# Linear attention on one core: half of relu(k) moved to GpSimd, its v copy in 32-bit elements, and new queue orders

## The chip, the cores and the metric

One core of one Trainium2 chip. The time is the device time of one execution in microseconds, the median of several runs. "Span" is the time from the first to the last instruction in the profile; in every run here whose time and span are both listed the span is 1.8 us shorter than the time. Engines: PE (TensorE), DVE (VectorE), ACT (ScalarE), POOL (GpSimd), SP (which issues the DMAs). The program gives each engine a queue of its own, and semaphores order the engines among themselves. A run is called slow when it is over 1.5% above the fastest of the same kernel, and fast otherwise.

## The reference

```python
# q, k, v: (1, 32, 2048, 128) bf16, so 32 heads of 2048 x 128
phi_q = where(q > 0, q + 1, exp(q)) + 1e-6
phi_k = where(k > 0, k + 1, exp(k)) + 1e-6
kv  = einsum("bhsd,bhse->bhde", phi_k, v)
z   = einsum("bhsd->bhd", phi_k)
num = einsum("bhqd,bhde->bhqe", phi_q, kv)
den = einsum("bhqd,bhd->bhq", phi_q, z)[..., None] + 1e-6
return num / den
```

Both kernels write phi(x) as relu(x) + (min(exp(x), 1) + 1e-6) and never add the two parts: each part has its own matmul, and both accumulate in PSUM. A column of ones beside v makes z come out of the same matmuls as kv.

## The kernel before

Per head h (16 tiles of 128 rows): exp of k on ACT (`ek`), min/add on DVE (`em`), relu of k on DVE (`rk`), a copy of v beside the ones on GpSimd (`v1`), 32 k-v matmuls (`kv`), a copy of kv out of PSUM on ACT (`kvs`). q is transposed on PE into PSUM (`T`), ACT takes exp (`eq`) and half of relu (`rqa`), DVE the other half (`rqb`) and min/add (`emq`). The numerator matmuls (`nA`, `nC`) use kvs; DVE takes the reciprocal of the denominator (`r`) and the product (`f`). DVE reads PSUM in `rqb`, `r` and `f`; `em`, `rk` and `emq` go from SBUF to SBUF.

```python
def emrk(h):
    s = h % 2
    add("DVE", f"em{h}", lambda e: e.tensor_scalar(
        em_sb[:, s], em_sb[:, s], 1.0, EPS, op0=ALU.min, op1=ALU.add), [f"ek{h}"])
    add("DVE", f"rk{h}", lambda e: e.tensor_scalar(
        rk_sb[:, s], k_sb[:, h % NI], 0.0, None, op0=ALU.max), [f"ldk{h}"] + ([f"kv{h - 2}"] if h >= 2 else []))

def v1(h):            # waits: ldv{h}, kv{h - 2}, nA{h - 3}
    ...
    add("POOL", f"v1{h}", lambda e: e.tensor_scalar(
        v1_sb[:, h % 2, :, 0:D], v_sb[:, h % NI].rearrange("p (j d) -> p j d", d=D), 1.0, 0.0,
        op0=ALU.mult, op1=ALU.add), dep)
# ... (rqa takes half of relu(q) in three heads of four, all of it in the fourth)
for i in range(NH):                   # the order of every queue
    eq(i)
    ...                               # the first head has its own order
        rqa(i)
    if i + 1 < NH:
        kvs(i + 1)
    if i + 2 < NH:
        ek(i + 2)
    if i >= 1:
        f(i - 1, "A")                 # reciprocal and product of tiles 0 to 11
    rqb(i)
    emq(i)
    if i >= 1:
        f(i - 1, "C")                 # of tiles 12 to 15
    if i + 2 < NH:
        emrk(i + 2)
    if i + 1 < NH:
        T(i + 1)
    nA(i)
    nC(i)
    if i + 2 < NH:
        kv(i + 2)
```

Of the kernel before, what the change touches and what calls it, by code (L numbers as in the profile page):

```python
# [8 lines left out]
ENGINES = ("PE", "DVE", "ACT", "POOL", "SP")  # L9

# [5 lines left out]
class Program:  # L16



    def __init__(self, sem):  # L20
        self.sem = sem
        self.ops = {e: [] for e in ENGINES}
        self.where = {}
        self.count = {}
        self.sems = {}

    def add(self, eng, key, fn, deps=(), dma=None, inc=True):

        name = dma if dma is not None else eng
        if dma is not None or inc:  # L30
            self.count[name] = self.count.get(name, 0) + (16 if dma is not None else 1)
        if key is not None:
            assert key not in self.where, key
            assert dma is not None or inc
            self.where[key] = (name, self.count[name], eng, len(self.ops[eng]))
        self.ops[eng].append((fn, tuple(deps), name, (16 if dma is not None else 1) if (dma is not None or inc) else 0))
# [47 lines left out]
def _eps_pieces():  # L84

    import struct

    def bf(x):
        u = struct.unpack("<I", struct.pack("<f", x))[0]
        u = (u + 0x7FFF + ((u >> 16) & 1)) & 0xFFFF0000  # L90
        return struct.unpack("<f", struct.pack("<I", u))[0]

    a = bf(EPS / 128)
    b = bf(EPS - 126 * a)
    return a, b, bf(EPS - 126 * a - b)


def bass_standalone__linear_attn_elu__prompt_kernel(nc: bass.Bass, q: bass.AP, k: bass.AP, v: bass.AP, out: bass.AP):
    B, H, S, D = q.shape
    assert D == P and S == 16 * P  # L100
    NT = S // P
    NH = B * H
    bf16, fp32 = mybir.dt.bfloat16, mybir.dt.float32
    N = NT * D
    NC = D + 1
    NI = 8
    NO = 6
    LAG = 2
# [4 lines left out]
    with ExitStack() as es:  # L113
# [11 lines left out]
        k_sb, q_sb, v_sb = sb([P, NI, N]), sb([P, NI, N]), sb([P, NI, N])  # L125
        em_sb, rk_sb = sb([P, 2, N]), sb([P, 2, N])
        v1_sb = sb([P, 2, NT, NC])
        emq_sb, rq_sb = sb([P, 2, N]), sb([P, 2, N])
        kvs_sb = sb([P, 2, NC])
        rden_sb = sb([P, 2, NT], fp32)  # L130
        o_sb = sb([P, NO, NT, D])
        ident, ones, epsr, one1 = sb([P, P]), sb([P, P]), sb([P, 3]), sb([P, 1])
        xT = alloc(nc.psum_tensor, [P, N], bf16)
# [3 lines left out]
        CO = 4 * 512  # L137

        def slot(t):
            if t < 12:  # L140
                return 512 * (t // 3) + NC * (t % 3)
            return CO + 512 * ((t - 12) // 2) + NC * ((t - 12) % 2)

        pr = Program(sem)
        add = pr.add


# [9 lines left out]
        for s in range(2):  # L157
            add("DVE", f"v1ones{s}", lambda g, s=s: g.memset(v1_sb[:, s, :, D:NC], 1.0))


        def load(name, dst, src, h, freed):
            dep = [f"{f}{h - NI}" for f in freed] if h >= NI else []
            add("SP", f"ld{name}{h}", lambda e: e.dma_start(
                dst[:, h % NI].rearrange("p (j d) -> p j d", d=D), rows(src, h)), dep, dma=f"{name}{h % NI}")

        def loads(h):
            load("k", k_sb, kf, h, ["ek", "rk"])
            load("q", q_sb, qf, h, ["T"])
            load("v", v_sb, vf, h, ["v1"])

        def store(h):
            s = h % NO
            if h < NH - 1:
                add("SP", f"st{h}", lambda e: e.dma_start(rows(of, h), o_sb[:, s]), [f"fA{h}", f"fC{h}"], dma=f"o{s}")
            else:
                add("SP", None, lambda e: e.dma_start(rows(of, h)[:, 0:12, :], o_sb[:, s, 0:12]), [f"fA{h}"], dma=f"o{s}")
                add("SP", f"st{h}", lambda e: e.dma_start(rows(of, h)[:, 12:NT, :], o_sb[:, s, 12:NT]), [f"fC{h}"],
                    dma=f"o{s}")

        for h in range(min(NI, NH)):  # L180
            loads(h)
        for h in range(NH + LAG):
            if h + NI < NH:
                loads(h + NI)
            if h >= LAG:
                store(h - LAG)


        def ek(h):
            add("ACT", f"ek{h}", lambda e: e.activation(em_sb[:, h % 2], k_sb[:, h % NI], ACT.Exp),  # L190
                [f"ldk{h}"] + ([f"kv{h - 2}"] if h >= 2 else []))

        def eq(h):
            add("ACT", f"eq{h}", lambda e: e.activation(emq_sb[:, h % 2], xT[:, :], ACT.Exp),  # L194
                [f"T{h}"] + ([f"nC{h - 2}"] if h >= 2 else []))

        def split(h):
            return h % 4 != 3

        def rqa(h):  # L200
            n = N // 2 if split(h) else N
            add("ACT", f"rqa{h}", lambda e: e.activation(rq_sb[:, h % 2, 0:n], xT[:, 0:n], ACT.Relu),  # L202
                [f"T{h}"] + ([f"nC{h - 2}"] if h >= 2 else []))

        def rqb(h):
            if split(h):
                add("DVE", f"rqb{h}", lambda e: e.tensor_scalar(  # L207
                    rq_sb[:, h % 2, N // 2:], xT[:, N // 2:], 0.0, None, op0=ALU.max),
                    [f"eq{h}"] + ([f"nC{h - 2}"] if h >= 2 else []))

        def rqs(h):
            return [f"rqa{h}"] + ([f"rqb{h}"] if split(h) else [])

        def kvs(h):
            add("ACT", f"kvs{h}", lambda e: e.activation(kvs_sb[:, h % 2], kv_ps, ACT.Copy),  # L215
                [f"kv{h}"] + ([f"nC{h - 2}"] if h >= 2 else []))

        def emrk(h):
            s = h % 2
            add("DVE", f"em{h}", lambda e: e.tensor_scalar(  # L220
                em_sb[:, s], em_sb[:, s], 1.0, EPS, op0=ALU.min, op1=ALU.add), [f"ek{h}"])
            add("DVE", f"rk{h}", lambda e: e.tensor_scalar(  # L222
                rk_sb[:, s], k_sb[:, h % NI], 0.0, None, op0=ALU.max), [f"ldk{h}"] + ([f"kv{h - 2}"] if h >= 2 else []))

        def emq(h):
            s = h % 2
            add("DVE", f"emq{h}", lambda e: e.tensor_scalar(  # L227
                emq_sb[:, s], emq_sb[:, s], 1.0, EPS, op0=ALU.min, op1=ALU.add), [f"eq{h}"])

        def v1(h):  # L230
            dep = [f"ldv{h}"]
            if h >= 2:
                dep += [f"kv{h - 2}"]
            if h >= 3:
                dep += [f"nA{h - 3}"]
            add("POOL", f"v1{h}", lambda e: e.tensor_scalar(  # L236
                v1_sb[:, h % 2, :, 0:D], v_sb[:, h % NI].rearrange("p (j d) -> p j d", d=D), 1.0, 0.0,
                op0=ALU.mult, op1=ALU.add), dep)

        def T(h):  # L240
            def f(e):
                for j in range(NT):
                    ins = e.transpose(xT[:, j * P:(j + 1) * P], q_sb[:, h % NI, j * D:(j + 1) * D], ident[:])  # L243
                return ins
            add("PE", f"T{h}", f, [f"ldq{h}", "ident"] + (([f"eq{h - 1}"] + rqs(h - 1)) if h else []))

        def kv(h):
            def f(e):
                for j in range(NT):
                    for part, src in ((0, em_sb), (1, rk_sb)):  # L250
                        ins = e.matmul(kv_ps, lhsT=src[:, h % 2, j * D:(j + 1) * D], rhs=v1_sb[:, h % 2, j, :],  # L251
                                       start=(j + part == 0), stop=(j == NT - 1 and part == 1))
                return ins
            add("PE", f"kv{h}", f, [f"em{h}", f"rk{h}", f"v1{h}", "v1ones0", "v1ones1"] + ([f"kvs{h - 1}"] if h else [])
                + ([f"fC{h - 3}"] if h >= 3 else []))

        def num(h, tiles, bank, n, e):
            s = h % 2
            e.matmul(_ap(o_ps[:, :], slot(tiles[0]) + D, [[NC, n]]), lhsT=ones[:], rhs=epsr[:, 0:n], start=True, stop=False,  # L259
                     skip_group_check=True)  # L260
            for t in tiles:
                o = o_ps[:, slot(t):slot(t) + NC]
                e.matmul(o, lhsT=emq_sb[:, s, t * P:(t + 1) * P], rhs=kvs_sb[:, s, :], start=False, stop=False,  # L263
                         skip_group_check=True)
                ins = e.matmul(o, lhsT=rq_sb[:, s, t * P:(t + 1) * P], rhs=kvs_sb[:, s, :], start=False, stop=True,  # L265
                               skip_group_check=True)
            return ins

        def nA(h):
            def f(e):  # L270
                for b in range(4):
                    ins = num(h, range(3 * b, 3 * b + 3), b, 3, e)
                return ins
# [3 lines left out]
        def nC(h):  # L277
            def f(e):
                num(h, (12, 13), 4, 2, e)
                return num(h, (14, 15), 5, 2, e)  # L280
# [126 lines left out]
```

## Time and profile before

| | before |
|---|---|
| time, median of 4 runs | 200.88 us (199.35 to 201.48) |
| span of the profiled execution | 197.3 us |
| busy: PE, DVE, ACT, POOL | 170.6, 161.6, 160.0, 68.4 us |
| period, from one kv copy to the next | 5.52 to 5.53 us in every head from the fourth |
| first numerator matmul | 19.6 us |

From the page of the kernel before: the span, the busy time of each engine, and the chain of work that ended last, by engine (a q at the end means the engine's sequencer; "issue" is time in which the engine waited for nothing that the profile shows).

```profile
span 197.3 us, 6384 instructions
...
PE 170.6 (86%) x2842; PEld 160.5 (81%) x2842; DVE 161.6 (82%) x254; ACT 160.0 (81%) x129; POOL 68.4 (35%) x38
...
ACT 37%; PE 33%; DVE 22%; DMA 3%; issue 2%; POOL 1%; SPq 0%
```

No engine is full and the chain wanders over three of them. That points to a loop of waits rather than an amount of work. The view of waits names its joints (who waited for whom, us in total, times, longest): L220 is min/add of k, L190 exp of k, L215 the kv copy, L251 the k-v matmuls.

```profile
DVE la L220 <- ACT la L190: 27.4, 32, 7.1
ACT la L215 <- PE la L251: 23.0, 25, 4.0
```

The timeline of ACT alone over one period (start us, duration us, what, and the idle time before it):

```profile
84.71 0.28 ACT L215 ACTIVATE la<-la 128x129 bf16<-128x129 f32 x1 [0.77 <-PE la L251]
84.89 1.90 ACT L190 ACTIVATE la<-la 128x2048 bf16<-128x2048 bf16 x1
86.69 1.87 ACT L194 ACTIVATE la<-la 128x2048 bf16<-128x2048 bf16 x1
88.44 1.03 ACT L202 ACTIVATE la<-la 128x1024 bf16<-128x1024 bf16 x1
90.24 0.28 ACT L215 ACTIVATE la<-la 128x129 bf16<-128x129 f32 x1 [0.77 <-PE la L251]
```

The kv copy (L215) waits for the k-v matmuls, and the next exp of k (L190) stands right behind it in ACT's queue. That exp feeds min/add and relu of k on DVE, those feed the next k-v matmuls, and those the next kv copy: 1.80 + 0.61 + 0.69 + 2.04 us and a copy of 0.2 to 0.3 us make 5.3 to 5.4 us, and the handovers from engine to engine the rest of the 5.5.

The timeline of DVE for one head (L222 relu of k, L293 reciprocal, L299 product, L207 half relu of q, L227 min/add of q):

```profile
92.35 0.69 DVE L220 TENSOR_SCALAR la<-la 128x2048 bf16<-128x2048 bf16 x1 [0.28 <-ACT la L190]
92.96 0.69 DVE L222 TENSOR_SCALAR la<-la 128x2048 bf16<-128x2048 bf16 x1
93.56 0.23 DVE L293 RECIPROCAL la<-la 128x12 f32<-128x12 f32 x1
93.82 1.76 DVE L299 TENSOR_TENSOR la<-la 128x1536 bf16<-128x1536 f32 x1
95.49 0.68 DVE L207 TENSOR_SCALAR la<-la 128x1024 bf16<-128x1024 bf16 x1
96.09 0.68 DVE L227 TENSOR_SCALAR la<-la 128x2048 bf16<-128x2048 bf16 x1
96.69 0.17 DVE L293 RECIPROCAL la<-la 128x4 f32<-128x4 f32 x1
96.90 0.69 DVE L299 TENSOR_TENSOR la<-la 128x512 bf16<-128x512 f32 x1
```

Durations overlap, so what an operation costs is the distance from its start to the next start: 0.60 for a min/add, 0.26 and 0.21 for the two small reciprocals. The one GpSimd operation of this head:

```profile
93.33 2.06 POOL L236 TENSOR_SCALAR la<-la 128x2048 bf16<-128x2048 bf16 x1 [3.46 <-PE la L265]
```

It starts while relu of k is still running and needs 2.06 us; undisturbed, as in the first heads, it needs 1.90. It lies under the product, and no DVE operation from SBUF to SBUF starts while it runs, here or in any other head.

### The profile page before, as it was taken

Reading aid. Unit: us, or ns where it says so; the run is one execution under the profiler, and the core shown is the slowest. Engines: PE = TensorE matmul, PEld = TensorE weight load, DVE = VectorE, ACT = ScalarE, POOL = GpSimd, SP = SyncE. Lnnn points to the kernel's source line nnn. Section 1 sums busy time; section 2 is a strip of 40 time slices with the busy share of each in tenths; the row PEclk is TensorE's granted clock in tenths of the full one; section 3 lists DMA queues with packets and bytes.
Section 4 is the critical chain, followed back from the end, with each engine's and each line's share of the span. In section 5 each row is a group of like instructions: output and inputs, shape, how many; then the busy total and the mean of one; then the engine's idle time right before and its main releaser. Section 6 shows DMA issues by size and latency. Waiting matters only on the chain.

```text
span 197.3 us, 6384 instructions
## 1 busy us (share of the span) xinstructions
PE 170.6 (86%) x2842; PEld 160.5 (81%) x2842; DVE 161.6 (82%) x254; ACT 160.0 (81%) x129; POOL 68.4 (35%) x38
## 2 busy tenths in 40 slices
PE   6948999988898899988898889988898889988850
PEld 6938889888897889888897889888897889988850
DVE  0213899899989999899989999899989999899774
ACT  4563789988898889988898889988898889998530
POOL 1333343322344444332344444432344444431000
PEclk9997999999999999999999999999999999999985
DMA  6999999999999999999999999999999622222133
GB/s 228 346 418 411 412 404 407 410 404 416 416 411 422 412 416 419 411 420 414 414 420 413 419 418 414 419 414 417 416 415 394 246 116 110 106 106 105 61 130 137
DMA packets 18603, 67.52 MB, mean 342 GB/s; under 512 B 2064, under 2 KB 2192, under 8 KB 18576
## 3 DMA queue, kind: packets, MB, share of 16 engines
q1 hardware_dynamic: 18576, 67.12, 84.4%
q8 instruction: 22, 0.36, 0.7%
q14 instruction: 5, 0.04, 0.1%
HBM read 50.33 MB, written 16.78 MB: 340 GB/s over the span
## 4 chain that ended last, share of the span: by engine, by line
ACT 37%; PE 33%; DVE 22%; DMA 3%; issue 2%; POOL 1%; SPq 0%
ACT la L190 21%; PE la L251 18%; DVE la L299 9%; ACT la L202 6%; ACT la L194 6%; DVE la L220 6%; PE la L243 5%; PE la L263 5%; PE la L265 5%; DVE la L222 4%; DMA la<-in_v_dram 3%; ACT la L215 3%; DVE la L207 2%; DVE la L293 1%; POOL la L236 1%
## 5 line engine op out<-in xcount | busy, mean ns | idle before, releaser
L236 POOL TENSOR_SCALAR la<-la 128x2048 bf16<-128x2048 bf16 x32 | 67.7, 2116 | 109.1 <-PE la L265 97.5
L299 DVE TENSOR_TENSOR la<-la 128x1536 bf16<-128x1536 f32 x64 | 78.4, 1224 | 2.2
L251 PE MATMUL la<-la 128*128 128x129 bf16 x1024 | 65.3, 222 | 5.7 <-DVE la L222 5.4
L251 PEld LDWEIGHTS la<-la 128*128 128x128 bf16 x1024 | 59.7, 98 | 10.2 <-DVE la L222 7.1
L265 PE MATMUL la<-la 128*128 128x129 bf16 x512 | 66.7, 221 | 0.0
L263 PE MATMUL la<-la 128*128 128x129 bf16 x512 | 66.6, 220 | 0.0
L194 ACT ACTIVATE la<-la 128x2048 bf16<-128x2048 bf16 x32 | 59.8, 1869 | 3.7 <-PE la L243 3.7
L190 ACT ACTIVATE la<-la 128x2048 bf16<-128x2048 bf16 x32 | 60.9, 1902 | 1.9 <-DMA la<-in_k_dram 1.9
L265 PEld LDWEIGHTS la<-la 128*128 128x128 bf16 x512 | 49.8, 97 | 0.0
L263 PEld LDWEIGHTS la<-la 128*128 128x128 bf16 x512 | 47.6, 98 | 0.0
L243 PE MATMUL la<-la 128*128 128x128 bf16 x512 | 35.0, 222 | 12.7 <-DVE la L207 11.5
L220 DVE TENSOR_SCALAR la<-la 128x2048 bf16<-128x2048 bf16 x32 | 22.2, 694 | 27.4 <-ACT la L190 27.4
L243 PEld LDWEIGHTS la<-la 128*128 128x128 bf16 x512 | 29.6, 99 | 18.0 <-DVE la L207 15.5
L202 ACT ACTIVATE la<-la 128x1024 bf16<-128x1024 bf16 (+1 forms) x32 | 39.6, 1238 | 0.0
L259 PE MATMUL la<-la 128*128 128x3 bf16 (+1 forms) x192 | 32.5, 169 | 2.2 <-DVE la L227 2.2
L215 ACT ACTIVATE la<-la 128x129 bf16<-128x129 f32 x32 | 9.0, 280 | 23.0 <-PE la L251 23.0
L222 DVE TENSOR_SCALAR la<-la 128x2048 bf16<-128x2048 bf16 x32 | 22.0, 687 | 0.0
L227 DVE TENSOR_SCALAR la<-la 128x2048 bf16<-128x2048 bf16 x32 | 21.8, 683 | 0.0
L259 PEld LDWEIGHTS la<-la 128*128 128x128 bf16 x192 | 19.0, 99 | 2.4 <-DVE la L227 2.4
L207 DVE TENSOR_SCALAR la<-la 128x1024 bf16<-128x1024 bf16 x24 | 16.3, 681 | 0.0
L293 DVE RECIPROCAL la<-la 128x12 f32<-128x12 f32 x64 | 12.9, 201 | 2.5 <-PE la L265 2.5
L308 PE MATMUL la<-la 128*128 128x120 bf16 x90 | 7.6, 268 | 1.5 <-POOL la L149 1.5
(13 smaller groups left out, 9.9 us busy)
## 6 DMA issues: line engine op xcount, KB each, us to landing
la<-in_k_dram SPq DMA_DIRECT2D x32, 512.0 KB, 15.0
la<-in_q_dram SPq DMA_DIRECT2D x32, 512.0 KB, 15.0
la<-in_v_dram SPq DMA_DIRECT2D x32, 512.0 KB, 15.2
out_dram<-la SPq DMA_DIRECT2D x31, 512.0 KB, 15.1
out_dram<-la SPq DMA_DIRECT2D x1, 384.0 KB, 2.3
out_dram<-la SPq DMA_DIRECT2D x1, 128.0 KB, 2.1
```

Of the source, the lines that this page charges most:

```text
L190: add("ACT", f"ek{h}", lambda e: e.activation(em_sb[:, h % 2], k_sb[:, h % NI], ACT.Exp), [f"ldk{h}"] + ([f"kv{h - 2}"] if h >= 2 else []))
L194: add("ACT", f"eq{h}", lambda e: e.activation(emq_sb[:, h % 2], xT[:, :], ACT.Exp), [f"T{h}"] + ([f"nC{h - 2}"] if h >= 2 else []))
L202: add("ACT", f"rqa{h}", lambda e: e.activation(rq_sb[:, h % 2, 0:n], xT[:, 0:n], ACT.Relu), [f"T{h}"] + ([f"nC{h - 2}"] if h >= 2 else []))
L220: add("DVE", f"em{h}", lambda e: e.tensor_scalar(em_sb[:, s], em_sb[:, s], 1.0, EPS, op0=ALU.min, op1=ALU.add), [f"ek{h}"])
L222: add("DVE", f"rk{h}", lambda e: e.tensor_scalar(rk_sb[:, s], k_sb[:, h % NI], 0.0, None, op0=ALU.max), [f"ldk{h}"] + ([f"kv{h - 2}"] if h ...
L236: add("POOL", f"v1{h}", lambda e: e.tensor_scalar(v1_sb[:, h % 2, :, 0:D], v_sb[:, h % NI].rearrange("p (j d) -> p j d", d=D), 1.0, 0.0, o ...
L243: ins = e.transpose(xT[:, j * P:(j + 1) * P], q_sb[:, h % NI, j * D:(j + 1) * D], ident[:])
L251: ins = e.matmul(kv_ps, lhsT=src[:, h % 2, j * D:(j + 1) * D], rhs=v1_sb[:, h % 2, j, :], start=(j + part == 0), stop=(j == NT - 1 and par ...
L259: e.matmul(_ap(o_ps[:, :], slot(tiles[0]) + D, [[NC, n]]), lhsT=ones[:], rhs=epsr[:, 0:n], start=True, stop=False, skip_group_check=True)
L263: e.matmul(o, lhsT=emq_sb[:, s, t * P:(t + 1) * P], rhs=kvs_sb[:, s, :], start=False, stop=False, skip_group_check=True)
L265: ins = e.matmul(o, lhsT=rq_sb[:, s, t * P:(t + 1) * P], rhs=kvs_sb[:, s, :], start=False, stop=True, skip_group_check=True)
L299: add("DVE", f"f{which}{h}", lambda e: e.tensor_tensor(out=_ap(o_sb[:, :, :, :], ob + t0 * D, [[n * D, nb], [D, n], [1, D]]), in0=_ap(o_ps ...
```

## The change

The intent is to take work from DVE and ACT and to reorder every queue. The v copy was on GpSimd before, in 16-bit elements, and stays there. The new orders are irregular from head to head; below they are called annealed. The core of the diff; the operations live on in the new code with other names (`em`, `rkd` and `rkp` for the two halves of relu(k), `n` for the numerator), and what is only renamed is cut.

```diff
-    NI = 8
-    NO = 6
+NI, NO, NE, NR, NV, NQ, NK = 7, 12, 2, 2, 2, 2, 2      # input buffers, output buffers, ...
+HALVES = ((0, 8), (8, 16))                             # head 0: loads, transposes, exps, v copy in halves
+RKP = (8, 8, ... 8)      # tiles of relu(k) on GpSimd, every head
+NA = (8, 8, ... 8)       # tiles of relu(q) on ACT; before: 8, 8, 8, 16
+ORDER = {                # ... cut: one period of each queue is shown
+    "PE":   ... n2.0 T4.0 n2.1 kv4.0 n3.0 T5.0 n3.1 kv5.0 ...
+    "DVE":  ... r5.0 f5.0 emq6.0 rkd8.0 em8.0 r5.1 rqb7 f5.1 r6.0 emq7.0 f6.0 rkd9.0 em9.0 r6.1 rqb8 f6.1 ...
+    "ACT":  ... eq4.0 kvs4 rqa4 ek6.0 eq5.0 kvs5 rqa5 ek7.0 ...
+    "POOL": ... v17.0 v18.0 rkp7.0 rkp8.0 rkp9.0 v19.0 rkp10.0 v110.0 rkp11.0 v111.0 v112.0 rkp13.0 rkp12.0 ...
+    "SP":   ... loads up to seven heads ahead, stores up to twelve heads late ...
+}
-            add("DVE", f"rk{h}", ... rk_sb[:, s], k_sb[:, h % NI], 0.0, None, op0=ALU.max ...
+                add("DVE", f"rkd{h}.{i}", ... rk_sb[:, h % NR, a:b], k_sb[:, h % NI, a:b], 0.0, None, op0=ALU.max ...
+                add("POOL", f"rkp{h}.{i}", ... rk_sb[:, h % NR, a:b], k_sb[:, h % NI, a:b], BIG, 0.0, op0=ALU.min, op1=ALU.max ...
-            add("POOL", f"v1{h}", lambda e: e.tensor_scalar(... 1.0, 0.0, op0=ALU.mult, op1=ALU.add), dep)
+                add("POOL", f"v1{h}.{i}", lambda e, a=a, b=b: e.tensor_copy(
+                    v1_sb[:, h % NV, a:b, 0:D].bitcast(i32), v_sb[:, h % NI, a:b].bitcast(i32)), ...
```

For the 32-bit copy the rows of v1 became one element wider, 130 for 129. The k-v product was already one PE operation per head and stays so. The last head's numerator and store are split in three.

## The prediction

> **What bounds the kernel now.** Page of the profile: span 197.3 us (timed 200.87: 3.5 us lie outside), PE busy 86%, DVE 82%, ACT 81%, POOL 35%. The timeline between 70 and 110 us repeats every 5.53 us per head, and the chain of waits shows the loop that sets this: exp of k on ACT 1.80, then on DVE min/add 0.61 and relu of k 0.69, then 32 k-v matmuls 2.04, then the kv copy on ACT 0.2 to 0.3, behind which the next exp of k is queued: 5.5 us. The view of waits agrees: ACT waits 23.0 us for those matmuls, DVE 27.4 us for the exp. DMA is 103% busy until 150 us but only runs ahead; after the start no engine waits for it. The first numerator matmul comes at 19.6 us; from the last head's first one to the end are about 7 us: 19.6 + 31 x 5.52 + 7 = 198.
>
> **What the change does.**
> - Queue order: exp of k is no longer behind the kv copy of the head just before, but one of two heads before; the transposes run two heads ahead of the numerator. This opens the 5.5 us loop (two periods for about 6 us of work): the main gain.
> - DVE, by starts in the timeline: now 0.61+0.60+0.26+1.67+0.60+0.60+0.21+0.65 = 5.2 us per head, 4.6 in every fourth. Half of relu(k) goes (-0.27), the exception too (+0.15 on average): 4.95 per head, from 5.05.
> - ACT: the eight full relus of q (1877 ns) become halves (1025 ns): -6.8 us; then about 4.7 us per head.
> - PE: same work, 1.86 + 0.90 + 1.98 = 4.75 us per head.
> - POOL: v copy as 1024 32-bit elements and 1024 elements of relu(k). From 1.90 us per 2048 undisturbed elements I estimate 1.0 us each, so about 2 to 2.3 us per head, as now. [...]
> - DMA: 67.1 MB at about 415 GB/s is 162 us, 5.05 per head. Stores may lag 12 heads, so it should stay just off the path.
>
> New period: DVE 4.95 if packed; with some bubbles I expect 5.1 to 5.15. Start: halves and the reordered ACT queue bring the first numerator to about 15.5 us (v is queued late: kv0 not before 11 us). Tail: half relu, three groups and stores, about 6.3 us. Span 15.5 + 31 x 5.13 + 6.3 = 181; plus 3.5: **184.5 us**, 8 in 10 between 179 and 192. Chances: faster 0.95, within 2% 0.03, slower 0.02.
>
> **What would show it.** Period 5.1 in the timeline; ACT's wait for k-v matmuls nearly gone; DVE above 88% busy and PE above 92%; first numerator near 15.5 us; half relu(k) on DVE about 0.42 us, both POOL operations near 1.0 us.
>
> **What would make it wrong.** [...] In this trace POOL's copy grows from 1.90 to 2.40 us when it meets one; DVE's operations never start inside a POOL one, so DVE's side is untested. Two POOL operations per head at new phases could block min/add or relu(k) by up to 1 us each and bring the period back to 5.4 (190 us). Also: loads queued behind stores in a full DMA.

The sum came to 15.5 + 31 x 5.13 + 6.3 = 181, and with 3.5 to 184.5 us. "One", in "when it meets one", is a DVE operation from SBUF to SBUF. That such an operation could be blocked by up to 1 us was my estimate, from the 1.0 us that I had estimated for a GpSimd operation; the trace of before shows only GpSimd's side, its copy at up to 2.40 us for 1.90.

## The result

178.52 us (median of 4 runs, 177.36 to 179.61) against 200.88. The ratio is 0.889, 95% interval 0.882 to 0.896; a ratio here is the mean time of one kernel's fast runs over that of the other's fast runs of the same rounds, so not quite the ratio of the medians. The predicted 184.5 was 6 us too long, and its range, from 179, just missed the result. Of the signs that it named, the vanished wait, half relu(k) at 0.42 us, GpSimd's operations near 1.0 us (1.04) and DVE above 88% busy (89%) came; the period of 5.1 us, the first numerator at 15.5 us (17.8) and PE above 92% (91%) did not.

The page of the changed kernel:

```profile
span 177.8 us, 6416 instructions
...
PE 161.9 (91%) x2842; PEld 158.1 (89%) x2842; DVE 158.4 (89%) x266; ACT 154.4 (87%) x131; POOL 71.5 (40%) x71
...
PE 43%; DVE 20%; DMA 18%; issue 5%; SPq 4%; ACT 4%; POOL 3%; DVEq 0%; POOLq 0%
```

Line numbers now: L308 exp of k, L311 min/add of k, L314 half relu of k on DVE, L318 the other half on GpSimd, L322 v copy, L329 k-v matmuls, L334 kv copy, L345 min/add of q, L352 half relu of q, L373 reciprocal, L380 product. The two waits of before, in the view of waits:

```profile
DVE la L311 <- ACT la L308: 3.1, 2, 1.7
ACT la L334 <- PE la L329: 1.0, 3, 0.5
```

27.4 and 23.0 us have become 3.1 and 1.0: the loop is gone. Of the 31 distances from one kv copy to the next, 24 are under 4.9 us, mostly 4.72 or 4.73; between 40 and 60 us the view by windows has PE and ACT busy for all of 20.00 us (stretch, its length, busy time of PE, PEld (PE's weight loads), DVE, ACT and POOL, granted clock, DMA):

```profile
40.00:60.00 20.00, 20.00 (x365) 19.86 (x364) 19.73 (x33) 20.00 (x18) 10.43 (x10) 1.00 1.03 408
```

The timeline of DVE in such a head:

```profile
51.97 0.18 DVE L373 RECIPROCAL la<-la 128x4 f32<-128x4 f32 x1
52.07 0.66 DVE L352 TENSOR_SCALAR la<-la 128x1024 bf16<-128x1024 bf16 x1
52.65 0.68 DVE L380 TENSOR_TENSOR la<-la 128x512 bf16<-128x512 f32 x1
53.25 0.22 DVE L373 RECIPROCAL la<-la 128x12 f32<-128x12 f32 x1
53.39 0.63 DVE L345 TENSOR_SCALAR la<-la 128x2048 bf16<-128x2048 bf16 x1
53.93 1.75 DVE L380 TENSOR_TENSOR la<-la 128x1536 bf16<-128x1536 f32 x1
55.59 0.42 DVE L314 TENSOR_SCALAR la<-la 128x1024 bf16<-128x1024 bf16 x1
55.93 0.69 DVE L311 TENSOR_SCALAR la<-la 128x2048 bf16<-128x2048 bf16 x1
```

By starts: 0.10 + 0.58 + 0.60 + 0.14 + 0.54 + 1.66 + 0.34 + 0.60 = 4.56 us (the last from other heads, as here the next operation waits for the numerator), where the prediction had 4.95. Between a reciprocal and its product stands an operation that needs neither, and the reciprocals cost 0.10 and 0.14 instead of 0.21 and 0.26.

But six heads take between 5.2 and 5.8 us. One of them, the 21st distance with 5.57, is not GpSimd's doing: ACT's queue there has half relu of q ahead of the kv copy, and e6 and e10 below have the same 5.57 in the same place. In two others a product also waits for the store that frees its output buffer: 0.86 us at 83.57 us, in the head of the first line below, and 0.53 at 158.23. For these five, two places in DVE's timeline, and then GpSimd's at the same time:

```profile
85.24 1.11 DVE L311 TENSOR_SCALAR la<-la 128x2048 bf16<-128x2048 bf16 x1
...
90.66 1.26 DVE L314 TENSOR_SCALAR la<-la 128x1024 bf16<-128x1024 bf16 x1
```

```profile
84.76 2.49 POOL L322 COPY la<-la 128x1024 int32<-128x1024 int32 x2 [3.45 <-PE la L329]
...
90.57 1.08 POOL L318 TENSOR_SCALAR la<-la 128x1024 bf16<-128x1024 bf16 x1 [2.31 <-PE la L329]
```

At 90.57 GpSimd starts its half relu; at 90.66 DVE's half relu, 0.42 us long when alone, is issued and ends at 91.92, 0.27 us after GpSimd's end at 91.65. It goes the other way too: in the kernel before, each v copy from the fifth head on starts while relu of k runs on DVE, ends 1.75 to 1.76 us after that relu's end and takes 1.99 to 2.40 us for 1.90. The two exclude each other in these traces, whichever starts first. In the profile the shut-out time of DVE is not idle time: it is counted as busy time of the DVE operation, here 1.26 us for 0.42.

The 19 kept traces say more than these two lines. In them 197 of DVE's operations from SBUF to SBUF are over 0.3 us longer than usual, 11 of them in the changed kernel and none in the kernel before. Every one began while a GpSimd operation ran, and every one ended at the same distance after that operation's end: 0.54 to 0.55 us with 2048 elements, 0.28 with 1024. They waited for its end; they were not merely slowed. DVE's work from PSUM never grew: the longest product took 1.76 us and the longest half relu of q 0.69 us in every kernel, though that half relu began under a GpSimd operation, with over 0.35 us of it to go, 23 times in the changed kernel alone.

The theory going in (A): the queue order opens the loop and is the main gain; the work moved to GpSimd makes room on DVE; a GpSimd operation shuts DVE out while it runs. Rivals: B, the moved work is the main gain; C, neither part gains alone.

### The profile page after: what moved, and what is told of

The parts are those of the page before. It is cut to its first block, busy times and chain, and to the rows that moved or that the text cites. A ratio compares the mean times of both kernels' runs of the same rounds, so it can differ in the third digit from the quotient of the medians.

```text
span 177.8 us, 6416 instructions
## 1 busy us (share of the span) xinstructions
PE 161.9 (91%) x2842; PEld 158.1 (89%) x2842; DVE 158.4 (89%) x266; ACT 154.4 (87%) x131; POOL 71.5 (40%) x71
## 4 chain that ended last, share of the span: by engine, by line
PE 43%; DVE 20%; DMA 18%; issue 5%; SPq 4%; ACT 4%; POOL 3%; DVEq 0%; POOLq 0%
PE la L329 17%; DMA la<-in_k_dram 11%; PE la L364 9%; PE la L366 8%; PE la L340 8%; DVE la L380 8%; DMA out_dram<-la 7%; SPq L296 4%; DVE la L314 4%; DVE la L311 3%; DVE la L352 2%; ACT la L343 2%; DVE la L345 2%; POOL la L318 2%; POOL la L322 2%
## 5 line engine op out<-in xcount | busy, mean ns | idle before, releaser
L380 DVE TENSOR_TENSOR la<-la 128x1536 bf16<-128x1536 f32 (+2 forms) x65 | 77.7, 1199 | 2.0 <-DMA out_dram<-la 1.4
L366 PE MATMUL la<-la 128*128 128x129 bf16 x512 | 69.2, 222 | 0.0
L364 PE MATMUL la<-la 128*128 128x129 bf16 x512 | 69.1, 221 | 0.0
L329 PE MATMUL la<-la 128*128 128x129 bf16 x1024 | 64.0, 219 | 2.0 <-ACT la L349 1.4
L343 ACT ACTIVATE la<-la 128x2048 bf16<-128x2048 bf16 (+1 forms) x33 | 60.1, 1825 | 6.5 <-PE la L366 6.0
L308 ACT ACTIVATE la<-la 128x2048 bf16<-128x2048 bf16 (+1 forms) x33 | 61.3, 1860 | 2.1 <-DMA la<-in_k_dram 1.9
L329 PEld LDWEIGHTS la<-la 128*128 128x128 bf16 x1024 | 59.9, 97 | 2.7 <-DVE la L278 1.5
L318 POOL TENSOR_SCALAR la<-la 128x1024 bf16<-128x1024 bf16 x32 | 36.1, 1137 | 44.1 <-PE la L329 33.5
L322 POOL COPY la<-la 128x1024 int32<-128x1024 int32 (+1 forms) x33 | 35.3, 1076 | 44.0 <-PE la L329 22.4
L349 ACT ACTIVATE la<-la 128x1024 bf16<-128x1024 bf16 x32 | 32.6, 1019 | 2.5 <-PE la L340 2.5
L311 DVE TENSOR_SCALAR la<-la 128x2048 bf16<-128x2048 bf16 (+1 forms) x33 | 23.3, 706 | 3.1 <-ACT la L308 3.1
L314 DVE TENSOR_SCALAR la<-la 128x1024 bf16<-128x1024 bf16 x32 | 18.0, 566 | 7.4 <-DMA la<-in_k_dram 7.3
L345 DVE TENSOR_SCALAR la<-la 128x2048 bf16<-128x2048 bf16 (+1 forms) x33 | 22.3, 677 | 0.4 <-ACT la L343 0.4
L352 DVE TENSOR_SCALAR la<-la 128x1024 bf16<-128x1024 bf16 x32 | 21.3, 667 | 0.7 <-ACT la L343 0.7
L373 DVE RECIPROCAL la<-la 128x12 f32<-128x12 f32 (+2 forms) x65 | 12.8, 198 | 2.2 <-PE la L366 1.4
L334 ACT ACTIVATE la<-la 128x129 bf16<-128x129 f32 x32 | 9.0, 281 | 1.0 <-PE la L329 1.0
(14 smaller groups left out, 13.5 us busy)
```

Of the source, the lines that this page charges most:

```text
L308: add("ACT", f"ek{h}.{i}", lambda e, a=a, b=b: e.activation(em_sb[:, h % NE, a:b], k_sb[:, h % NI, a:b], ACT.Exp), [f"ldk{h}.{i}"] + freed ...
L311: add("DVE", f"em{h}.{i}", lambda e, a=a, b=b: e.tensor_scalar(em_sb[:, h % NE, a:b], em_sb[:, h % NE, a:b], 1.0, EPS, op0=ALU.min, op1=AL ...
L318: add("POOL", f"rkp{h}.{i}", lambda e, a=a, b=b: e.tensor_scalar(rk_sb[:, h % NR, a:b], k_sb[:, h % NI, a:b], BIG, 0.0, op0=ALU.min, op1=A ...
L322: add("POOL", f"v1{h}.{i}", lambda e, a=a, b=b: e.tensor_copy(v1_sb[:, h % NV, a:b, 0:D].bitcast(i32), v_sb[:, h % NI, a:b].bitcast(i32)), ...
L329: ins = e.matmul(kv_ps, lhsT=src[:, j], rhs=v1_sb[:, h % NV, j, 0:NC], start=(j + part == 0), stop=(j == NT - 1 and part == 1))
L343: add("ACT", f"eq{h}.{i}", lambda e, a=a, b=b: e.activation(emq_sb[:, h % NQ, a:b], xT[:, a:b], ACT.Exp), [f"T{h}.{i}"] + freed(NQ, h, ("n ...
```

## The experiments

Seventeen kernels ran. Four give a wrong result and are marked. Times are medians of all runs; e1, e15, e17 and e19 have one slow run each, which the ratios leave out. "Before" ran in the same rounds with medians of 200.1 to 201.0 us. Differences of 1 to 2 us between single medians are no more than runs of one kernel scatter.

| run | what | us | ratio to before |
|---|---|---|---|
| e8 | annealed orders, old operations | 198.5 | 0.987 |
| e2 | before, with the moved work | 207.5 | 1.043 |
| e7 | changed, v copy in 16 bits | 202.4 | 1.016 |
| e4 | changed, relu(k) all on DVE | 180.9 | 0.909 |
| e13 | before, GpSimd short (wrong) | 200.0 | 1.002 |
| e11 | orders with old operations, GpSimd short (wrong) | 181.7 | 0.911 |
| e6 | changed, GpSimd short (wrong) | 174.3 | 0.867 |
| e9 | changed, regular order | 186.1 | 0.925 |
| e10 | e9 with gates on GpSimd | 174.5 | 0.868 |
| e3 | changed, reciprocal and product adjacent | 194.7 | 0.979 |
| e14 | e10, reciprocal and product adjacent | 176.8 | 0.885 |
| e1 | before, two entries of ACT's queue swapped | 211.8 | 1.062 |
| e12 | e1, GpSimd short (wrong) | 198.9 | 0.995 |
| e15 | e10, 14 output buffers | 176.9 | 0.879 |
| e18 | e15, gates from the fifth head | 175.9 | 0.880 |
| e17 | e18, first head whole | 175.6 | 0.879 |
| e19 | e10, memsets first | 175.4 | 0.877 |

### The parts of the change apart: e8, e2, e7, e4

**e8**, the orders with the operations of before:

```diff
-RKP = (8, ... 8)
-NA = (8, 8, ... 8)
+RKP = (0,) * 32
+NA = (8, 8, 8, 16) * 8
-    e.tensor_copy(v1_sb[...].bitcast(i32), v_sb[...].bitcast(i32))
+    e.tensor_scalar(v1_sb[...], v_sb[...], 1.0, 0.0, op0=ALU.mult, op1=ALU.add)
```

> The changed kernel with the operations of the kernel before (relu of k whole on DVE, v copied in 16 bits on GpSimd, relu of q whole on ACT in every fourth head) in the annealed orders. Theory A (orders are the main gain): DVE needs about 4.55 + 0.27 us per head, less 0.58 in every fourth; ACT's fourth head costs 0.9 more; time 180 to 186 us. Theory C (each part alone is worth nothing or costs, as the two edits of the kernel before did, and only the fit of orders and operations gains): above 192 us, with DVE operations lengthened to 1.3 us or more by GpSimd's 1.9 us copies.

198.51 us. Theory A's 180 to 186 is wrong as it stood; C was right for this run. After the first, its heads take anything from 4.72 to 6.93 us, and the timelines of DVE and GpSimd show why:

```profile
69.64 2.38 DVE L309 TENSOR_SCALAR la<-la 128x2048 bf16<-128x2048 bf16 x1
```

```profile
69.45 2.03 POOL L320 TENSOR_SCALAR la<-la 128x2048 bf16<-128x2048 bf16 x1 [2.54 <-PE la L327]
```

A min/add issued 0.19 us after the v copy began lasts 2.38 us.

**e2**, the kernel before with the moved work:

```diff
-                rk_sb[:, s], k_sb[:, h % NI], 0.0, None, op0=ALU.max), ...)
+                rk_sb[:, s, 0:N // 2], k_sb[:, h % NI, 0:N // 2], 0.0, None, op0=ALU.max), ...)
+        def rkp(h):  # POOL
+            ... rk_sb[:, h % 2, N // 2:], k_sb[:, h % NI, N // 2:], 3.4028234663852886e38, 0.0, op0=ALU.min, op1=ALU.max
-            add("POOL", f"v1{h}", lambda e: e.tensor_scalar(... 1.0, 0.0, ...), dep)
+            add("POOL", f"v1{h}", lambda e: e.tensor_copy(....bitcast(i32), ....bitcast(i32)), dep)
```

> The kernel before with only the moved work: half of relu of k and the 32-bit v copy on GpSimd, queue orders as before. Theory A: the loop loses half a relu of k, about 0.27 us, so the period is about 5.25 us and the time about 192.5 us (191 to 195), and the loop can still be seen in ACT's wait for the k-v matmuls. Theory B: the moved work is the main gain, time below 186 us. If GpSimd holds DVE up in this order, the time is above 195 us.

207.53 us: slower than before, as the last clause allowed. In the old order GpSimd's half relu is released by the end of a k-v product, at 94.45 us for example, and DVE's min/add of q is issued 0.15 us later and lasts 1.44 us for 0.68. It happens in three heads of four; in the fourth it is relu of k, 1.26 us for 0.42. The period is 5.7 to 6.1 us. (v1's rows are one element wider here too.) B is dead; the shortened loop that A expected cannot be seen under this.

**e7**, the changed kernel with the v copy in 16 bits (the last edit of e8 alone):

> The changed kernel with only the v copy back in 16 bits: GpSimd 3.0 us per head for 2.1, its longest operation 1.9 for 1.04 us. Theory A (a GpSimd operation shuts DVE out for its whole length): more and longer heads, 5 to 12 us more than 178.5, that is 183 to 191 us, DVE operations of 2 us and more. Rival (GpSimd has slack, 40% busy): within 1.5 us.

202.42 us, beyond even theory A's range: everything that the change gained is lost. The operations, in DVE's timeline and GpSimd's:

```profile
66.43 2.07 DVE L345 TENSOR_SCALAR la<-la 128x2048 bf16<-128x2048 bf16 x1
...
70.08 1.64 DVE L314 TENSOR_SCALAR la<-la 128x1024 bf16<-128x1024 bf16 x1
```

```profile
66.06 1.90 POOL L322 TENSOR_SCALAR la<-la 128x2048 bf16<-128x2048 bf16 x1
69.55 1.90 POOL L322 TENSOR_SCALAR la<-la 128x2048 bf16<-128x2048 bf16 x1 [1.59 <-PE la L329]
```

GpSimd is far from full, but each v copy bars DVE for 1.90 us instead of 1.04, and a DVE operation that meets one can lose nearly all of that: a min/add issued at 58.16 us, 0.12 us into a copy, takes 2.38 us for 0.69. The copy's 2048 16-bit elements take 1.90 us (as a multiply and add; a plain 16-bit copy was not run), the same bytes as 1024 32-bit elements 1.04 us, and 1024 16-bit elements of relu(k) 1.04 us too: by my estimate from these times, 0.84 ns per element and 0.18 us per operation. A rival is that the k-v matmuls simply wait longer for a slower copy: in the view of waits they wait 4.4 us for GpSimd in e7 and 2.7 us in e8, a small part of the loss. DVE's busy time, for the same operations, is 182.9 us in e7 against 158.4 in the changed kernel: 24.5 us, about what the run lost.

**e4**, the changed kernel with relu(k) whole on DVE:

```diff
-RKP = (8, ... 8)
+RKP = (0,) * 32
```

> The changed kernel with all of relu(k) on DVE and none on GpSimd; orders otherwise kept. Theory A (the order is the main gain, the moved half makes room on DVE): DVE needs 4.55 + 0.27 = 4.8 us per head, just over PE's 4.72; the long heads caused by GpSimd blocking DVE get fewer; time 178 to 183 us. Theory B (moved work essential): above 188 us.

180.94 us, as A had it: most periods are 4.81 to 5.0 us. The half relu moved to GpSimd, the first item of the title, is worth 2.4 us by the medians and about 4 by the ratios; the 32-bit copy 24 us, given the rest.

### Is it GpSimd shutting DVE out? e13, e11, e6, e9, e10

The three runs with GpSimd short cut its operations to one tile from the third head on, so that the same waits and semaphores stay and only their length goes:

```diff
-    v1_sb[:, h % 2, :, 0:D], v_sb[:, h % NI]...            # e13 (and e12); e6 and e11 likewise,
+    v1_sb[:, h % 2, 0:(NT if h < 2 else 1), 0:D], ...      # in e6 for the half relu too
```

**e13**, on the kernel before:

> Wrong result on purpose: the kernel before with its v copy cut to one tile from the third head. If GpSimd has no part in its 5.52 us period (the loop exp of k - min/add - relu - k-v matmuls - k-v copy sets it, and no DVE operation is lengthened): within 0.5% of the kernel before. [...]2% or more faster.

(The condition cut from the text was that GpSimd has a part in the period after all.) 200.04 us, ratio 1.002 (0.993 to 1.011), period 5.52 and 5.53 as before. The period of before has nothing of GpSimd in it.

**e11**, on e8:

> Wrong result on purpose: the run 'orders only' (198.5 us) with the v copy on GpSimd cut to one tile from the third head. Theory A (the annealed orders open the loop; with the old operations the gain is lost again to GpSimd shutting DVE out[...]): periods of 4.8 us, 5.5 in every fourth head where ACT does all of relu(q); time 180 to 185 us. Rival (orders alone are worth little even then): above 192 us.

181.69 us for 198.51, within A's range: most periods are 4.72 to 4.91, and 5.55 in every fourth head, where ACT does all of relu(q). So the orders do open the loop, with old operations too; with GpSimd's 1.9 us copy whole, the gain is lost again, and DVE is busy 177.0 us for 157.8.

**e6**, on the changed kernel:

> Wrong result on purpose: from the third head GpSimd copies one tile of v and makes one tile of relu of k; all else as changed. Theory A: without GpSimd's 1 us operations DVE is hardly ever shut out, the long heads (5.5 us, seven of them) shrink to those caused by stores: time 171 to 175 us. Rival (long heads come from the DMA order): 177 to 179 us.

174.25 us for 178.52. GpSimd's length still costs the changed kernel about 4.3 us. A shorter GpSimd also delivers v and relu(k) sooner; e10 keeps its work whole and so tells the two apart.

**e9 and e10** keep GpSimd's work whole. e9 gives every head from the fourth the same order; e10 adds gates, two extra waits that let GpSimd start only when DVE has begun a stretch of work from PSUM:

```diff
 # e9, per head, DVE:  r(h).0 emq(h+1) f(h).0 em(h+3) rkd(h+3) r(h).1 rqb(h+2) f(h).1
 #     PE: n(h).0 T(h+2) n(h).1 kv(h+2)      POOL: rkp(h) v1(h)
 # e10, as well:
 def gate(name, h):
-    return []
+    if h < 6:
+        return []
+    return [f"emq{h - 2}.0"] if name == "rkp" else [f"r{h - 3}.1"]
```

> The changed kernel with the same order in every head on DVE, PE and GpSimd from the fourth head (reciprocal, min/add of q, product, min/add and half relu of k, reciprocal, half relu of q, product), no gates. If the annealed irregular order matters only through the gap behind the reciprocals, the period is 4.72 and the time 172 to 179 us. [...]the period is over 5.2 and the time above 186 us.

> The run before with one thing more: from the seventh head GpSimd's half relu of k waits for DVE's min/add of q (so it runs under DVE's 1.67 us product from PSUM) and its v copy waits for DVE's second reciprocal (so it runs under half relu of q and the second product, 1.2 us, both from PSUM). Theory A (a GpSimd operation shuts out DVE's SBUF-to-SBUF operations while it runs): no DVE min/add or relu of k is lengthened any more, nearly all periods are 4.72 to 4.75 us, PE-bound, time 170 to 175 us. If the long heads of the changed kernel come from stores and loads instead: time 176 to 180 us with the same 5.5 us heads.

(The condition cut from the text on e9 was that the regular order puts GpSimd's starts on the same DVE operations in head after head, as in e3.) e9: 186.06 us, right at the edge of the second branch in time, with a mean period of 5.1 us, under the 5.2 named. The periods alternate, 4.72 and 5.69 us, through most of the run: in every second head GpSimd's start falls on a DVE operation. e10: 174.51 us (174.31 to 174.79), the fastest correct kernel and equal to e6, where GpSimd does next to nothing. One head of e10 on DVE (lines are two further down than in the changed kernel), and GpSimd at the same time:

```profile
75.04 0.18 DVE L375 RECIPROCAL la<-la 128x4 f32<-128x4 f32 x1
75.14 0.66 DVE L354 TENSOR_SCALAR la<-la 128x1024 bf16<-128x1024 bf16 x1
75.72 0.68 DVE L382 TENSOR_TENSOR la<-la 128x512 bf16<-128x512 f32 x1
76.32 0.22 DVE L375 RECIPROCAL la<-la 128x12 f32<-128x12 f32 x1
76.46 0.63 DVE L347 TENSOR_SCALAR la<-la 128x2048 bf16<-128x2048 bf16 x1
77.00 1.75 DVE L382 TENSOR_TENSOR la<-la 128x1536 bf16<-128x1536 f32 x1
```

```profile
75.29 1.04 POOL L324 COPY la<-la 128x1024 int32<-128x1024 int32 x1 [1.80 <-DVE la L375]
77.17 1.04 POOL L320 TENSOR_SCALAR la<-la 128x1024 bf16<-128x1024 bf16 x1 [0.84 <-DVE la L347]
```

Both GpSimd operations take their undisturbed 1.04 us, lying under half relu of q and the products, which read PSUM; nothing on DVE is longer than alone. The same work, one wait more per operation, 11.6 us less than e9. Some luck is in the 174.5: its four runs agree within 0.5 us, but its near relatives below (e15, e18, e17, e19) come to 175.4 to 176.9 us, so the gate is worth 9 to 12 us.

### How much does DVE need? e3 and e14

This is the term of the prediction that was off. **e3** moves each reciprocal of the changed kernel directly ahead of its product:

```diff
-    ... r6.0 emq7.0 f6.0 ... r6.1 rqb8 f6.1 ...
+    ... emq7.0 r6.0 f6.0 ... rqb8 r6.1 f6.1 ...
```

> The changed kernel with each reciprocal put directly ahead of the product that uses it (before: about half of them have another operation between). Theory A (my 4.95 us of DVE per head was too high because the annealed order puts another operation into the gap between reciprocal and product, 0.21 to 0.26 us from start to start as a pair, 0.09 to 0.14 with something between): DVE needs about 4.8 to 4.95 us per head again, becomes the fullest engine, period about 4.9, time 180 to 184 us against 178.5. Theory B (the gap is not on the path, PE's 4.72 us binds): time within 0.7% of 178.5 us.

194.71 us, far over A's 180 to 184. The rest is GpSimd shutting DVE out again: DVE is busy 178.0 us for 158.4 in the changed kernel, with the same operations. DVE, and GpSimd:

```profile
71.66 1.54 DVE L311 TENSOR_SCALAR la<-la 128x2048 bf16<-128x2048 bf16 x1
```

```profile
71.62 2.48 POOL L318 TENSOR_SCALAR la<-la 128x1024 bf16<-128x1024 bf16 x2 [3.26 <-PE la L329]
```

GpSimd is released by the end of a k-v product, at a fixed point of the period, and once the new order puts a DVE operation from SBUF there, it meets it in head after head: six periods in a row of 5.71 to 5.74 us. So e3 does not price the pair. **e14** does, with e10's gates set anew:

```diff
-    ... r(h).0 emq(h+1) f(h).0 em(h+3) rkd(h+3) r(h).1 rqb(h+2) f(h).1
+    ... emq(h+1) r(h).0 f(h).0 em(h+3) rkd(h+3) rqb(h+2) r(h).1 f(h).1
-    return [f"emq{h - 2}.0"] if name == "rkp" else [f"r{h - 3}.1"]
+    return [f"r{h - 3}.0"] if name == "rkp" else [f"rkd{h}.0" if h > 6 else "em6.0"]
```

> The gated kernel (174.5 us) with each reciprocal directly ahead of its product, the gates moved so that GpSimd still runs only under DVE's work from PSUM. It prices the adjacent pair alone. By starts in the traces DVE needs 0.60+0.26+1.67+0.60+0.34+0.60+0.21+0.60 = 4.88 us per head against 4.55: period 4.88 to 4.95, time 179 to 182 us (the size that the prediction had for DVE). If the pair alone cost what the ungated pairs run showed, it would be 190 us or more.

From the ninth distance on the period is 4.88 us in nearly every head, exactly the sum, and DVE has no gap there; the time, 176.80 us, is below the range that I had put on it. One reason is that I had compared with an ideal e10: over the 31 distances between kv copies the profiled e14 takes 149.6 us and the profiled e10 147.1, of which e10 loses 1.1 us in one head of 5.79 us, waiting for a store, that e14 does not have. Another is that most of e14's first eight distances are 4.70 to 4.77. The 2.3 us between the two times are within the scatter of e10's relatives, so the price of the pair is read from the period. In e14's timeline of DVE each product waits behind its reciprocal:

```profile
72.06 0.17 DVE L375 RECIPROCAL la<-la 128x4 f32<-128x4 f32 x1
72.27 0.69 DVE L382 TENSOR_TENSOR la<-la 128x512 bf16<-128x512 f32 x1
...
73.48 0.23 DVE L375 RECIPROCAL la<-la 128x12 f32<-128x12 f32 x1
73.74 1.76 DVE L382 TENSOR_TENSOR la<-la 128x1536 bf16<-128x1536 f32 x1
```

So DVE at 4.88 us, near the predicted 4.95, was true of an order that the changed kernel does not have. At 4.56 it lies under the 4.72 of the full ACT and PE.

### The loop of before: e1 and e12

```diff
-            if i + 1 < NH:
-                kvs(i + 1)
             if i + 2 < NH:
                 ek(i + 2)
+            if i + 1 < NH:
+                kvs(i + 1)
```

> The kernel before with one swap in ACT's queue: exp of k of the head after next goes ahead of the k-v copy of the next head; nothing else. Theory A (the loop exp of k - min/add - relu of k - k-v matmuls - k-v copy sets 5.52 us per head, and the order opens it): the period falls to 5.05 to 5.25 us, where DVE (5.05 us per head) or the loop numerator - division - relu of q - transpose (about 5.15 us) binds; time 188 to 192 us. Theory B (the loop is only how the chain happens to run; DVE's amount of work sets the period): period stays at 5.4 or more, time within 2% of 200.9 us.

> Wrong result on purpose: the kernel before with exp of k ahead of the k-v copy (211.8 us) and the v copy on GpSimd cut to one tile from the third head. Theory A (the swap opens the 5.5 us loop; its loss came from DVE being shut out for up to 1.6 us): periods 5.2 to 5.3 us in three heads of four and 5.5 to 6.2 in the fourth, none of 7; time 190 to 199 us. Rival (the swap makes a worse loop of its own): 205 us or more.

e1: 211.84 us, neither theory. In one of its slowest heads, 7.40 us, a min/add lasts 2.30 us because a GpSimd copy had started 0.15 us before it. e12, without that: 198.9 us, in A's range, but not in the shape that I gave it: the periods go round 5.24, 6.20, 4.62 and 5.98 us, on average 5.51, the same as before. The swap frees exp of k but puts the kv copy, on which the second part of the numerator and its reciprocal wait, behind it. In the fourth head, with its 1.87 us relu of q on ACT, DVE's reciprocal waits 1.6 us for that copy (6.20 us), and two heads on ACT waits 1.2 us for transposes (5.98); that costs what the others gain. The loop is therefore shown by e13 and e11 (it is not GpSimd, and the annealed orders open it), not by this swap.

### What is left: e15, e18, e17, e19

```diff
-NI, NO, ... = 7, 12, ...
+NI, NO, ... = 7, 14, ...                                                       # e15, e18, e17
+    if h < 4: return []                                                        # e18, e17: gates from the fifth head
+    if h == 5: return ["r2.0"] if name == "rkp" else ["rkd6.0"]
-    return HALVES if h == 0 else WHOLE
+    return WHOLE                                                               # e17
-    v1ones0 rkd0.0 em0.1 ...                                                   # e19: DVE's queue
+    v1ones0 v1ones1 eps0 eps1 eps2 ones rkd0.0 em0.1 ...
```

> The gated kernel with 14 output buffers for 12. Its trace still shows two heads of 5.6 to 5.8 us, and a tail, where the product waits for the store that frees its buffer. If that wait is the cause: both gone, 172 to 173.5 us. If the loads' arrival or the queue order is: same, 174.3 to 174.8 us.

The 5.79 us head of e10 where the product waited for a store was gone, but the time was 176.93 us, with fast runs from 174.76 to 177.31; the profiled execution lost 2.3 us in one early head, ahead of the gates, to a min/add of 1.40 and a half relu of 1.25 us.

> The gated kernel with 14 output buffers and with gates from the fifth head instead of the seventh. The 14-buffer run lost 2.3 us in one head, before the gates begin, where GpSimd shut DVE out (min/add 1.40, half relu 1.25 us). Theory A: with the gates earlier that cannot happen; the time is 171.5 to 174 us and the runs agree better than the 174.8 to 178.3 of the 14-buffer run. If load arrivals are what scatters: same scatter.

175.89 us, a miss: the collision of the early heads was gone, but runs still went from 173.67 to 176.27, and in the profiled one an exp of k in the middle waited 0.68 us for a load that had been 15.3 us on its way. So a late load can lengthen a head too; how much of the scatter it makes is not shown.

> The same kernel with the first head in one piece instead of halves (loads, transposes, exps, min/adds, v copy). It prices the halves: the first relu of q can start only when all of q is there and transposed. Expected 0.5 to 2 us longer than with halves, all before the first numerator matmul; no difference in the period of 4.72.

175.62 us: no cost can be seen. In the profile the first relu of q starts at 6.2 us, but the exp of k behind it starts at 7.2 us, against 8.0 in e18, where the load of k came later, and both reach the second exp of q at 13.5 to 13.6 us. The halves of the first head bring nothing that shows here.

> The gated kernel (174.5 us) with DVE's five small memsets at the front of its queue, where DVE is idle until 6.7 us; the annealed order has the ones of the second v buffer behind half relu of q of the second head, at 15.5 us. Theory: the second k-v product waits for that memset, 1.4 us; without it the first numerator starts near 16.7 us for 17.7, and the time is 0.3 to 1 us less, 173.5 to 174.2 us. Rival: the product waits for something else at the same time (half relu(k), v, the k-v copy) and starts where it did.

Inconclusive: 175.38 us (174.13 to 177.75), and the profiled run, 177.75, was slow. The first numerator came at 17.52 us for 17.73; its second k-v product started at 15.69 us, 0.1 us after the end of the first kv copy (15.30 us and 0.29), for which it must wait. The memset does not look like the main cause.

## Why the prediction was wrong

- **"the chain of waits shows the loop that sets this"**, 5.5 us per head, was right. The wait fell to 1.0 us, and with GpSimd made short the period of before did not move (e13) while the annealed orders reached 4.72 to 4.91 us in three heads of four (e11).
- **"New period: DVE 4.95 if packed; with some bubbles I expect 5.1 to 5.15"** is the step that failed. I took DVE's cost from starts of the old order, which include the wait of each product for its reciprocal, and so made DVE the engine that binds. The new order fills that gap behind 46 of the 65 reciprocals, behind both of the head in half of the heads, and DVE needs about 4.56 us there, not 4.95; ACT and PE, which I had at 4.7 and 4.75, are full at 4.72 and bind instead. From the first numerator of the first head to that of the last the trace has 152.15 us, 4.91 per head; I had 31 x 5.13 = 159.0. e14 shows 4.88 us for the old adjacency.
- **"bring the period back to 5.4"**, the risk, was right (GpSimd does hold DVE up: 1.26 us for 0.42) and in part real: it makes most of the step from 4.72 to the mean of 4.91 (4.76 in e6), and without GpSimd's length the kernel takes 4.3 us less (e6). I did not see that it also decides whether the change gains at all: with the copy in 16 bits the same order takes 202.4 us.
- **"as now"**, of GpSimd's load of 2 to 2.3 us per head, looked at the sum. It is the length of one operation that counts, 1.04 instead of 1.90 us. I had given the 32-bit copy no gain.
- **"the main gain"**, of the queue order, holds only together with the short copy (e8 198.5, e7 202.4 us).
- Four smaller terms. The first numerator came at 17.8 us, not 15.5 (why is open; the first k-v product started at 12.6 us, not 11, and e19 makes one cause unlikely). From the last head's first numerator to the end it took 7.9 us, not 6.3. The time outside the span is 1.8, not 3.5 us: I had subtracted a span from the median of other runs. The profiled run was 1.1 us over the median.

The stores, which the prediction had "just off the path", cost two waits of 1.4 us in all. The sum: 2.3 - 6.9 + 1.6 - 1.7 - 1.1 = -5.8, and 0.2 of rounding, for the 6.0 us between 184.5 and 178.5. It was luck that start and tail, 3.9 us too short, went against the period, 6.9 us too long; and the allowance for bubbles, 0.15 to 0.2 us, met the real 0.19 only on the wrong base.

Open: whether ACT or PE sets the 4.72, as both are full. The trace of e10 points to PE: from 61 to 80 us its matmuls start without a gap over 0.09 us, while ACT's exp of q takes 1.84 us from start to start ahead of the kv copy, which needs PE, and 1.77 in the one head where half relu of q follows it. No run tests this. Open too: which part of the new orders opens the loop, as only the whole was tried with success (e11); the late start; and how much of the 2 us scatter is load arrival.

## What to carry to other kernels

Before moving work to GpSimd, ask which of DVE's SBUF-to-SBUF operations it will meet, and for how long one operation bars them, here up to nearly its whole 1.04 or 1.90 us: shorten the operation (e7 to the changed kernel, 202.4 to 178.5 us), and tie its start to a stretch in which DVE reads PSUM (e9 to e10, 186.1 to 174.5 us), rather than to whatever frees its buffer. Here a DVE operation longer than its own minimum (2.38 us for 0.69) was a wait in disguise, which the view of waits does not show. Cost an engine from the order that it will run, not from the one that it ran: a small result used at once can cost more than its duration (0.21 us for 0.17 here).
